# Block-sorted attention with a gated MLP on one core: q and the attention output turned by DMA transposes

## The chip, the core and the metric

The kernel runs on one core of a Trainium2 chip. A core has five engines with an instruction queue each: PE (TensorE, matrix products, with its weight loads listed apart as PEld), DVE (VectorE), ACT (ScalarE), POOL (GpSimd) and SP (SyncE, here for starting DMAs only). Sixteen DMA engines move data between the device's memory (HBM) and the core's SBUF. PE writes its results to PSUM, 8 banks of 2 KB on each of 128 partitions, and DVE or ACT copy them out to SBUF. The metric is the device time of one execution in microseconds (us), less is better.

An engine works through its queue in order. An instruction that waits for a semaphore holds up all that stands behind it on the same engine, a DMA start on SP or POOL included.

## The reference

Four batches, eight heads, 768 positions, 64 numbers a head. A small matrix per head and batch, made doubly stochastic by five rounds, mixes the eight blocks of 96 positions of k and v; each block then attends within itself. The heads together are the input x of a gated MLP (gMLP).

```
def _attn_ref(q, k, v, sort_net) -> np.ndarray:
    ...
    P = sort_net
    for _ in range(5):
        P = P - np.max(P, axis=-1, keepdims=True)
        P = np.exp(P)
        P = P / (np.sum(P, axis=-1, keepdims=True) + 1e-09)
        P = P / (np.sum(P, axis=-2, keepdims=True) + 1e-09)
    ...
    k_sorted = np.einsum('bhij,bhjcd->bhicd', P, k_b).reshape(B, H, S, D)
    v_sorted = np.einsum('bhij,bhjcd->bhicd', P, v_b).reshape(B, H, S, D)
    ...
    scores = scale * np.matmul(q_b, k_sb.transpose(0, 1, 2, 4, 3))
    ...
    return np.matmul(attn, v_sb).reshape(B, H, S, D).astype(np.float32)

def _moe_ref(x, w_in, w_spatial, b_spatial, w_out) -> np.ndarray:
    h = np.maximum(x @ w_in, 0.0)
    u, v = (h[..., :d_ff // 2].copy(), h[..., d_ff // 2:].copy())
    ...
    v_n = (v - mu) / np.sqrt(var + 1e-06)
    v_s = np.einsum('ts,bsd->btd', w_spatial, v_n) + b_spatial[None, :, None]
    gated = u * v_s
    return (gated @ w_out).astype(np.float32)
```

Here B = 4, H = 8, S = 768, D = 64, d_model = 512 and d_ff = 1024. Inputs and output are float32; the kernel works in bf16 with float32 sums.

## The kernel before

The work is cut into units, one function `u_XX` each, and a long string ORDER lists their calls. That list alone sets the order of the instructions on every engine: the scheduler is told to keep it. The arguments of a unit follow after colons: usually the PSUM tile, the engine that copies the result out (A for ACT, D for DVE), the batch, the pair of heads, and the half of the blocks. hp is a pair of heads (four in all), ih a half of the eight blocks (384 positions).

The units, in the order of the data:

- L loads: q, k or v of a batch by one DMA on POOL's queue, cast to bf16 on the way, as 128 x 8 pieces of 384 numbers (a partition holds six neighbouring positions of each head); also the weights wv and wu (the two halves of w_in), ws (w_spatial) and wo (w_out). IN loads the sorting matrix by SP, and the first 64 partitions of batch 0's q in float32 (q_raw), which CQ casts on ACT and POOL.
- SK is one of the five normalizing rounds (ACT and DVE in turn), PR, P0, PC and PD spread the result into the mixing matrices pd of each batch, on PE, DVE, ACT and POOL.
- QT turns q of two heads on PE with the identity matrix, 12 products for a batch (ih = 2) or a half of the partitions (ih = 0 or 1), and a copy PSUM to SBUF into qT. KT does the same with pd in the identity's place, which gives the sorted K. VT and VX do batch 0's sorted V; for the others VM forms it, and VC moves it to blocks of 96 rows by eight DMAs on SP (vb from vm).
- SC computes scores of a pair of heads and a half (8 products) and their exponentials on ACT; AT the product with V (8 products) and, on DVE, the division by the row sum, into x_sb, 96 positions to a partition row.
- XT turns two chunks of x_sb by 8 transposes on PE, with a copy by DVE or ACT into xT. A batch needs four XT (two halves, two chunk pairs).
- WS turns w_spatial. VP and UP are the two halves of x @ w_in, LN and LA the normalization, SP the product with w_spatial and the gate (z and gt), OP the last product, with a copy to o_sb and a DMA on SP to the output. BB loads the bias b_bc.
- DM are products of zeros (of the tile warm) on PE early on.

x_sb is a ring of two tiles, qT one of five, the q loads one of two. PSUM is four tiles of two banks; `ps_tile` hands one out:

```
    def ps_tile(n, dt=FP32):
        return psum.tile([128, 2, 512 if dt == FP32 else 1024], dt, name=f"ps{n}", tag=f"ps{n}")
```

A unit that takes tile n waits until the last unit on it has been copied out.

Of the kernel before, what the change touches and what calls it, by code (L numbers as in the profile page):

```python
# [8 lines left out]
FP32 = mybir.dt.float32  # L9
BF16 = mybir.dt.bfloat16  # L10
# [11 lines left out]
QT:3:D:0:2:1 QT:1:A:0:1:1 QT:0:D:0:3:1 VT:2:A:3:1 SC:3:0:1:0 VX:1:D:2:0 AT:0:0:0:0 PD:1:0:4
VT:2:A:3:0 QT:1:A:0:0:1 VT:3:D:0:1 L:q:1:0:128 SC:2:0:1:1 VX:0:D:3:0 L:wo AT:1:0:2:0 VX:3:A:0:1
VX:0:A:3:1 AT:2:0:3:0 VT:3:A:1:1 VT:1:A:2:1 L:v:2:0:128 AT:0:0:1:0 SC:3:0:2:1 XT:2:D:0:0:1 SC:1:0:3:1
XT:0:D:0:0:0 L:k:2:0:128 VX:3:A:1:1 PD:1:4:8 WS:2:D:1 SC:1:0:0:1 WS:0:D:3 VX:3:A:2:1 L:q:2:0:128
WS:2:D:0 AT:1:0:1:1 WS:0:A:5 AT:3:0:0:1 VP:2:D:0:0:1 VM:1:A:1:2 VM:0:A:1:1 UP:3:A:0:0:0 VM:2:D:1:0
VM:1:A:1:3 VP:0:A:0:2 KT:3:A:1:2:2 KT:1:A:1:0:2 AT:2:0:3:1 UP:0:A:0:1:0 AT:3:0:2:1 KT:1:A:1:3:2
# [18 lines left out]
SP:1:D:2:2 AT:2:3:3:0 UP:3:A:3:1:1 UP:0:A:3:0:1 AT:1:3:1:0 SP:3:D:2:0 XT:2:A:3:0:0 XT:0:A:3:0:1
VP:1:A:3:4:5 VP:3:A:3:0:1 VP:2:A:3:2:3 LN:3:4:6 UP:0:A:3:0:0 LA:3:5 UP:1:A:3:1:0 LA:3:4 LN:3:0:4
LA:3:1 OP:3:A:2:1 OP:2:A:2:0 LA:3:2 OP:0:A:2:2 LA:3:3 LA:3:0 SP:1:D:3:2 SP:3:P:3:3 SP:2:D:3:1
SP:0:D:3:0 OP:1:A:3:1 OP:3:D:3:0 OP:2:A:3:2
# [12 lines left out]
def kernel(  # L62
# [12 lines left out]
    nc = tc.nc  # L75
# [3 lines left out]
    BLK = S // NB  # L79
# [44 lines left out]
    q_raw = const.tile([64, H, G * D], FP32, name="q_raw")  # L124
# [33 lines left out]

    def u_L(what, *a):
# [36 lines left out]

    def u_CQ(eng, hp):
        hp = int(hp)
        if ("q", 0) not in st:
            alloc(0, "q")  # L200
        o, i = st["q", 0][0:64, 2 * hp:2 * hp + 2], q_raw[:, 2 * hp:2 * hp + 2]
        if eng == "A":
            nc.scalar.copy(out=o, in_=i)  # L203
        else:
            nc.gpsimd.tensor_copy(out=o, in_=i)  # L205
# [356 lines left out]
```

## Time and profile before

| | us |
|---|---|
| three runs: median (lowest to highest) | 176.13 (174.57 to 176.19) |
| the profiled execution | 175.73 |
| its span, from the first to the last instruction | 173.7 |
| mean granted clock of PE in it | 0.953 of full |

All rows of the profile come from that one execution. Times in rows are microseconds from the start of the span, or mean nanoseconds where a row says so. The page cuts the span into 40 slices and gives the busy share of each engine in tenths, the clock that PE was granted (PEclk) and the DMA engines' share. A row of a group of instructions reads: line, engine, operation, output tile, input tiles and shape, count, then busy time and mean ns of one, then the idle time of the engine just ahead of them and what ended it. The chain of waits follows the work that ended last back through whatever released it; in order of time it lists start, duration and what ran. Matmuls are pipelined, so PE's cost of a unit is read from the chain, which counts from one start to the next, and not from the mean of one.

Sizes of DMAs are given as written to SBUF; a load with a cast reads twice that from HBM. In the row of a DMA issue, the last number is the time from the issue to the landing of the last byte.

### The profile page before, as it was taken

The numbers are of one execution on the slowest core, as the hardware profiler recorded it, in microseconds if no ns is written. First come the engines' busy times: TensorE is split into PE (matmuls) and PEld (weight loads), VectorE is DVE, ScalarE is ACT, GpSimd is POOL, SyncE is SP. The second block draws the span as 40 slices with busy tenths as digits, with TensorE's granted clock in tenths as the row PEclk, the third lists the DMA queues.
The fourth block names the chain that finished last, engine by engine and source line by source line (L and its number), as shares of the span: only waits on it lengthen the run. The fifth ranks groups of instructions, "written<-read, shape, count | busy, mean of one in ns | idle before, by whom it ended". The sixth has DMA issues, their size and how long they took to land.

```text
span 173.7 us, 4271 instructions
## 1 busy us (share of the span) xinstructions
PE 151.8 (87%) x1827; PEld 97.8 (56%) x1838; DVE 120.1 (69%) x252; ACT 93.5 (54%) x140; POOL 34.1 (20%) x42
## 2 busy tenths in 40 slices
PE   0096697999989999999999999999999999999570
PEld 0054586885865785656457556754566655455220
DVE  5277765568778888878876759888767759537420
ACT  4144574557896898043777660738644357620030
POOL 8285940911010000350000017200000000003000
PEclk9999975569999999999999999999999999999996
DMA  3999999999999990189253018100440000170044
GB/s 78 200 204 204 207 213 203 204 204 205 204 250 262 204 180 4 27 137 171 40 207 142 17 16 154 23 0 4 179 183 4 0 0 4 54 283 25 0 184 178
DMA packets 21025, 21.97 MB, mean 126 GB/s; under 512 B 912, under 2 KB 17808, under 8 KB 21008
## 3 DMA queue, kind: packets, MB, share of 16 engines
q0 software_dynamic: 14336, 11.80, 43.3%
q1 hardware_dynamic: 6672, 9.91, 19.9%
q8 instruction: 14, 0.23, 0.5%
q14 instruction: 3, 0.02, 0.0%
HBM read 24.78 MB, written 6.29 MB: 179 GB/s over the span
## 4 chain that ended last, share of the span: by engine, by line
PE 74%; DMA 9%; DVE 9%; issue 3%; ACT 2%; SPq 1%; ACTq 0%; DVEq 0%
PE ps L493 17%; PE ps L440 11%; PE ps L481 11%; PE ps L514 10%; PE ps L399 5%; PE ps L376 5%; DMA q_raw<-in_q_dram 4%; PE ps L303 3%; PE ps L421 3%; DMA vb<-vm 3%; PE ps L288 2%; PE ps L336 2%; PE ps L267 2%; DMA out_dram<-o_sb 2%; PE ps L348 1%
## 5 line engine op out<-in xcount | busy, mean ns | idle before, releaser
L384 ACT ACTIVATE ex<-ps 96x768 bf16<-96x768 f32 x32 | 24.7, 803 | 17.9 <-PE ps L376 17.5
L493 PE MATMUL ps<-wspT,v_sb 128*128 128x384 bf16 x192 | 33.2, 326 | 0.0
L505 POOL TENSOR_TENSOR gt<-z,u_sb 128x768 bf16<-128x768 f32 x6 | 9.8, 1638 | 100.4 <-DVE z L499 76.6
L493 PEld LDWEIGHTS <-v_sb 128*128 128x128 bf16 x192 | 18.1, 98 | 11.5
L514 PE MATMUL ps<-w_out_sb,gt 128*128 128x512 bf16 x92 | 21.7, 379 | 2.3 <-DVE gt L505 2.1
L481 PE MATMUL ps<-xT,w_in_sb 128*128 128x384 bf16 x128 | 23.1, 326 | 0.0
L499 DVE TENSOR_TENSOR z<-ps,b_bc 128x768 f32<-128x768 f32 x16 | 15.3, 955 | 11.3 <-PE ps L493 11.3
L407 DVE TENSOR_TENSOR x_sb<-ps,rec 96x512 bf16<-96x512 f32 x32 | 22.0, 687 | 1.1
L440 PE MATMUL ps<-w_in_sb,xT 128*128 128x512 bf16 x89 | 22.2, 379 | 0.4
L454 DVE BATCH_NORM_STATS2 stats<-v_sb 128x6 f32<-128x512 bf16 x24 | 16.3, 679 | 5.8 <-ACT v_sb L112 5.6
L106 ACT COPY o_sb<-ps 128x1024 f32<-128x1024 f32 x10 | 10.1, 1013 | 18.4 <-PE ps L514 14.3
L112 ACT ACTIVATE u_sb<-ps 128x768 bf16<-128x768 f32 x15 | 12.1, 809 | 7.8 <-PE ps L481 7.4
L514 PEld LDWEIGHTS <-gt 128*128 128x128 bf16 x96 | 9.0, 98 | 12.5 <-DVE gt L505 2.5
L481 PEld LDWEIGHTS <-w_in_sb 128*128 128x128 bf16 x128 | 11.8, 98 | 7.6
L288 PE MATMUL ps<-ident,q_in 128*64 128x128 bf16 (+1 forms) x240 | 8.4, 221 | 8.7 <-POOL q_in L205 8.7
L399 PE MATMUL ps<-vb,ex 96*128 96x65 bf16 x256 | 13.8, 201 | 1.7 <-issue 1.1
L399 PEld LDWEIGHTS <-ex 96*128 96x128 bf16 x256 | 12.1, 103 | 5.0 <-issue 1.9
L440 PEld LDWEIGHTS <-xT 128*128 128x128 bf16 x96 | 8.7, 97 | 9.2
L288 PEld LDWEIGHTS <-q_in 128*64 128x64 bf16 (+1 forms) x240 | 7.0, 120 | 9.6 <-ACT q_in L203 8.7
L376 PEld LDWEIGHTS <-kT 64*96 64x96 bf16 x256 | 8.2, 128 | 4.9 <-issue 3.7
L376 PE MATMUL ps<-qT,kT 64*96 64x96 bf16 x256 | 10.8, 219 | 0.1
L112 ACT ACTIVATE v_sb<-ps 128x1024 bf16<-128x1024 f32 (+1 forms) x9 | 8.4, 928 | 4.6 <-PE ps L440 4.6
(75 smaller groups left out, 200.6 us busy)
## 6 DMA issues: line engine op xcount, KB each, us to landing
out_dram<-o_sb SPq DMA_DIRECT2D x12, 512.0 KB, 2.8
k_in<-in_k_dram POOLq DMA_DIRECT2D x4, 768.0 KB, 17.4
v_in<-in_v_dram POOLq DMA_DIRECT2D x4, 768.0 KB, 14.8
vb<-vm SPq DMA_DIRECT2D x24, 99.0 KB, 2.8
q_in<-in_q_dram POOLq DMA_DIRECT2D x3, 768.0 KB, 18.3
wsp_nat<-in_moe_w_spatial_dram POOLq DMA_DIRECT2D x1, 1152.0 KB, 10.4
w_in_sb<-in_moe_w_in_dram POOLq DMA_DIRECT2D x2, 512.0 KB, 12.6
q_raw<-in_q_dram SPq DMA_DIRECT2D x1, 768.0 KB, 6.6
```

The costliest lines, as they stand in the source:

```text
L112: nc.scalar.activation(out=out, in_=in_, func=AF.Relu)
L288: nc.tensor.matmul(t[hh * 64:hh * 64 + 64, g * n:(g + 1) * n], lhsT=st["q", b][lo:lo + n, 2 * hp + hh, g * D:(g + 1) * D], rhs=ident[lo:lo ...
L376: nc.tensor.matmul(t[0:BLK, hh, ii * BLK:(ii + 1) * BLK], lhsT=kT[rows, i * BLK:(i + 1) * BLK], rhs=qT[rows, i * BLK:(i + 1) * BLK], start ...
L384: nc.scalar.activation(out=e[:, 0:2 * NI * BLK].rearrange("p (h c) -> p h c", h=2), in_=t[0:BLK, :, 0:NI * BLK], func=AF.Exp, scale=scale,)
L399: nc.tensor.matmul(t[:, hh, ii * VW:ii * VW + D + 1], lhsT=e[:, c:c + 128], rhs=vb[b % 2][:, ih * NI + ii, 2 * hp + hh, 0:D + 1], start=Tr ...
L407: nc.vector.tensor_mul(out=x_sb[:, :, hp * 128:hp * 128 + 128].rearrange("p i (h d) -> p h i d", h=2), in0=tv[:, :, :, 0:D], in1=_raw_ap(r ...
L440: nc.tensor.matmul(t[:, x, :], lhsT=st["xT", b][:, kc, n * 128:(n + 1) * 128], rhs=w_in_sb[:, kc, DH:DFF], start=(kc == 0), stop=(kc == KC ...
L454: nc.vector.bn_stats(out=stats, in_=v_sb[:, x, :])
L481: nc.tensor.matmul(t[:, x, 0:HW], lhsT=w_in_sb[:, kc, mc * 128:(mc + 1) * 128], rhs=st["xT", b][:, kc, ih * HW:(ih + 1) * HW], start=(kc = ...
L493: nc.tensor.matmul(t[:, x, 0:HW], lhsT=st["v_sb", b, n][:, mc * 128:(mc + 1) * 128], rhs=wspT[:, n, x * HW:(x + 1) * HW], start=(n == 0), ...
L499: nc.vector.tensor_add(out=z.rearrange("p (x c) -> p x c", x=2), in0=t[:, :, 0:HW], in1=b_bc.rearrange("p (x c) -> p x c", x=2),)
L514: nc.tensor.matmul(t[:, x, :], lhsT=st["gt", b, mc][:, c * 128:(c + 1) * 128], rhs=w_out_sb[:, mc, :], start=(mc == 0), stop=(mc == FC - 1),)
```

## The change

The following is done at once, with a new ORDER for all of it.

- The first half of batch 0's q is loaded by POOL's queue with a cast, as its first DMA (L:q:0:0:64). q_raw and CQ are gone.
- Batch 0's KT takes all 128 partitions in one unit (ih = 2) instead of two halves; PR puts both halves of its product into one bank.
- PSUM is one tile of eight banks, and a unit takes the bank n of its argument and the next. Units that need one bank may take an odd one, and the dependences follow from the banks that are touched.
- For batches 1 to 3, LQ loads q with 64 numbers to a piece, positions on partitions, by eight DMAs on POOL's queue, and QX turns the whole batch by one DMA transpose on SP into qT, which is now one tile for all heads, in a ring of two. The twelve QT of these batches are gone.
- For batches 1 to 3, XX turns a half of x by one DMA transpose on SP into an xT tile for that half (a ring of four). The twelve XT of these batches are gone. Batch 0 keeps XT and QT.
- Copies, gates and loads are spread anew over the engines and the list.

The diff, with a line or two of the list:

```diff
--- before.py
+++ after.py
@@ -14,39 +14,35 @@
 
 
 ORDER = """
-IN ID L:k:0:0:128 MK L:v:0:0:128 SX SK:0 L:wv SK:0 CQ:P:2 CQ:A:3 SK:0 QT:0:A:0:3:0 SK:0 QT:1:A:0:2:0
...
+L:q:0:0:64 ID IN SK:0 L:k:0:0:128 MK SK:0 SX SK:0 QT:0:A:0:1:0 QT:7:A:0:3:0 QT:1:A:0:2:0 SK:0
...
 """
 
 
@@ -98,8 +94,11 @@
     small = ctx.enter_context(tc.tile_pool(name="small", bufs=4))
     psum = ctx.enter_context(tc.tile_pool(name="psum", bufs=1, space=bass.MemoryType.PSUM))
 
+    ps = psum.tile([128, 8, 512], FP32, name="ps")
+    ps_bf = ps.rearrange("p x c -> p (x c)").bitcast(BF16).rearrange("p (x c) -> p x c", x=8)
+
     def ps_tile(n, dt=FP32):
-        return psum.tile([128, 2, 512 if dt == FP32 else 1024], dt, name=f"ps{n}", tag=f"ps{n}")
+        return (ps if dt == FP32 else ps_bf)[:, int(n):min(int(n) + 2, 8)]
 
     def copy(eng, out, in_):
         if eng == "A":
@@ -121,7 +120,6 @@
     p_t = const.tile([BH, 2, BH], BF16, name="p_t")
     sel = const.tile([BH, NI, 128], BF16, name="sel")
     m32 = const.tile([128, TB], FP32, name="m32")
-    q_raw = const.tile([64, H, G * D], FP32, name="q_raw")
     rowsum = const.tile([BH, NB], FP32, name="rowsum")
     colsum = const.tile([BH, NB], FP32, name="colsum")
     b_bc = const.tile([128, S], FP32, name="b_bc")
@@ -156,6 +154,35 @@
             in_=_raw_ap(src, b * H * S * D + lo * G * D, [[G * D, hi - lo], [S * D, H], [1, G * D]]),
         )
 
+    def u_LQ(b):
+        b = int(b)
+        st["q", b] = ld.tile([128, HP, G, 2, D], BF16, name="q_tok", tag="q")
+        for h in range(H):
+            nc.gpsimd.dma_start(
+                out=st["q", b][:, h // 2, :, h % 2],
+                in_=_raw_ap(q, (b * H + h) * S * D, [[D, 128], [128 * D, G], [1, D]]),
+            )
+
+    def u_QX(b):
+        b = int(b)
+        q_tile(b, 0)
+        nc.sync.dma_start_transpose(
+            out=st["qT", b].rearrange("p h (c x) -> p (h c) x", x=128),
+            in_=st["q", b].rearrange("p a c h d -> p (a c h d)"),
+        )
+
+    def u_XX(b, ih):
+        b, ih = int(b), int(ih)
+        nc.sync.dma_start_transpose(
+            out=x_tile(b, ih).rearrange("p k (i c) -> p (k i) c", c=BLK),
+            in_=st["x", b, ih].rearrange("p k i c -> p (k i c)"),
+        )
+
+    def x_tile(b, ih):
+        if ("xT", b, ih) not in st:
+            st["xT", b, ih] = att.tile([128, KC, HW], BF16, name="xT", tag="xT", bufs=4)
+        return st["xT", b, ih]
+
     def u_L(what, *a):
         if what in ("q", "k", "v"):
             load(what, *(int(x) for x in a))
@@ -172,7 +199,6 @@
 
     def u_IN():
         nc.sync.dma_start(out=p_all, in_=sort_net.rearrange("b h i j -> (b h) i j"))
-        nc.sync.dma_start(out=q_raw, in_=_raw_ap(q, 0, [[G * D, 64], [S * D, H], [1, G * D]]))
         nc.vector.memset(warm, 0.0)
         nc.vector.memset(eps_tile, 1e-6)
 
@@ -193,16 +219,6 @@
         nc.vector.tensor_copy(out=mask16, in_=m32)
         for n in range(NE):
             nc.vector.memset(ex[n][:, 2 * NI * BLK:], 0.0)
-
-    def u_CQ(eng, hp):
-        hp = int(hp)
-        if ("q", 0) not in st:
-            alloc(0, "q")
-        o, i = st["q", 0][0:64, 2 * hp:2 * hp + 2], q_raw[:, 2 * hp:2 * hp + 2]
-        if eng == "A":
-            nc.scalar.copy(out=o, in_=i)
-        else:
-            nc.gpsimd.tensor_copy(out=o, in_=i)
 
     def u_IV(n):
         n = int(n)
@@ -226,7 +242,7 @@
                 out=p_t.rearrange("p x y -> p (x y)"), in_=p_bf.rearrange("p i j -> p (i j)"))
 
     def u_PR(ps):
-        st["pr"] = ps_tile(ps)[:, :, 0:NI * BH].rearrange("p x (i y) -> p x i y", i=NI)
+        st["pr"] = ps_tile(ps)[:, 0, 0:NB * BH].rearrange("p (x i y) -> p x i y", x=2, i=NI)
         for ih in range(2):
             for ii in range(NI):
                 nc.tensor.matmul(
@@ -270,9 +286,9 @@
 
 
     def q_tile(b, hp):
-        if ("qT", b, hp) not in st:
-            st["qT", b, hp] = att.tile([128, S], BF16, name="qT", tag="qT", bufs=5)
-        return st["qT", b, hp]
+        if ("qT", b) not in st:
+            st["qT", b] = att.tile([128, HP, S], BF16, name="qT", tag="qT", bufs=2)
+        return st["qT", b][:, hp]
 
     def k_tile(b, hp):
         if ("kT", b, hp) not in st:
@@ -390,7 +406,7 @@
     def u_AT(ps, b, hp, ih):
         b, hp, ih = int(b), int(hp), int(ih)
         if ("x", b, ih) not in st:
-            st["x", b, ih] = att.tile([BLK, NI, DM], BF16, name="x_sb", tag="x", bufs=2)
+            st["x", b, ih] = att.tile([BLK, KC, NI, 128], BF16, name="x_sb", tag="x", bufs=2)
         e, x_sb = st["e", b, hp, ih], st["x", b, ih]
         t = ps_tile(ps)
         for hh in range(2):
@@ -405,27 +421,25 @@
         rec = small.tile([BLK, 2, NI], FP32, name="rec", tag="rec")
         nc.vector.reciprocal(out=rec, in_=tv[:, :, :, D])
         nc.vector.tensor_mul(
-            out=x_sb[:, :, hp * 128:hp * 128 + 128].rearrange("p i (h d) -> p h i d", h=2),
+            out=x_sb[:, hp].rearrange("p i (h d) -> p h i d", h=2),
             in0=tv[:, :, :, 0:D],
             in1=_raw_ap(rec, 0, [rec.ap[0], [NI, 2], [1, NI], [0, D]]),
         )
 
     def u_XT(ps, eng, b, ih, kp):
         b, ih, kp = int(b), int(ih), int(kp)
-        if ("xT", b) not in st:
-            st["xT", b] = att.tile([128, KC, S], BF16, name="xT", tag="xT", bufs=2)
         t = ps_tile(ps, BF16)
         for x in range(2):
             kc = 2 * kp + x
             for ii in range(NI):
                 nc.tensor.transpose(
                     t[:, 0, x * HW + ii * BLK:x * HW + (ii + 1) * BLK],
-                    st["x", b, ih][:, ii, kc * 128:(kc + 1) * 128],
+                    st["x", b, ih][:, kc, ii, :],
                     ident[0:BLK, 0:BLK],
                 )
         copy(
             eng,
-            st["xT", b][:, 2 * kp:2 * kp + 2, ih * HW:(ih + 1) * HW],
+            x_tile(b, ih)[:, 2 * kp:2 * kp + 2],
             t[:, 0, 0:S].rearrange("p (x c) -> p x c", x=2),
         )
 
@@ -439,7 +453,7 @@
             for kc in range(KC):
                 nc.tensor.matmul(
                     t[:, x, :],
-                    lhsT=st["xT", b][:, kc, n * 128:(n + 1) * 128],
+                    lhsT=x_tile(b, n // 3)[:, kc, n % 3 * 128:(n % 3 + 1) * 128],
                     rhs=w_in_sb[:, kc, DH:DFF],
                     start=(kc == 0), stop=(kc == KC - 1),
                 )
@@ -480,7 +494,7 @@
             for kc in range(KC):
                 nc.tensor.matmul(
                     t[:, x, 0:HW], lhsT=w_in_sb[:, kc, mc * 128:(mc + 1) * 128],
-                    rhs=st["xT", b][:, kc, ih * HW:(ih + 1) * HW],
+                    rhs=x_tile(b, ih)[:, kc],
                     start=(kc == 0), stop=(kc == KC - 1),
                 )
         relu(eng, st["u", b, m][:, :, ih * HW:(ih + 1) * HW], t[:, :, 0:HW])
```

On SP's queue, from the first copies of v to the first outputs, stood this before (vb is the sorted v of a batch in blocks, vm the same before the move):

```order
L363 DMA vb1_99<-vm1_97 96x1x528 x8
L180 DMA b_bc_82<-in_moe_b_spatial_dram 128x768
L363 DMA vb0_98<-vm0_96 96x1x528 x8
L522 DMA out_0_dram<-o_sb_1741 128x2x512
L522 DMA out_0_dram<-o_sb_1753 128x2x512
L522 DMA out_0_dram<-o_sb_1810 128x2x512
```

and this stands there now (q_tok is a batch's q as LQ loads it, x_sb a half of the attention output):

```order
L169 DMA_TRANSPOSE qT_889<-q_tok_814 128x24x128
L379 DMA vb1_99<-vm1_97 96x1x528 x8
L206 DMA b_bc_82<-in_moe_b_spatial_dram 128x768
L169 DMA_TRANSPOSE qT_1043<-q_tok_947 128x24x128
L379 DMA vb0_98<-vm0_96 96x1x528 x4
L176 DMA_TRANSPOSE xT_1202<-x_sb_998 128x16x96
L379 DMA vb0_98<-vm0_96 96x1x528 x4
L176 DMA_TRANSPOSE xT_1355<-x_sb_1107 128x16x96
L536 DMA out_0_dram<-o_sb_1473 128x2x512
L169 DMA_TRANSPOSE qT_1490<-q_tok_1278 128x24x128
L536 DMA out_0_dram<-o_sb_1502 128x2x512
```

The transposes of q stand ahead of the copies of v for the same batch, and the transpose of batch 2's q (the fourth row) stands ahead of those of batch 1's x.

On POOL's queue, from batch 1's q to batch 2's, stood this before:

```order
L154 DMA q_in_601<-in_q_dram 128x8x384
L171 DMA w_out_sb_90<-in_moe_w_out_dram 128x4x512
L154 DMA v_in_686<-in_v_dram 128x8x384
L154 DMA k_in_741<-in_k_dram 128x8x384
L251 TENSOR_TENSOR pd1_93<-mask16_84,prep_sb_91 128x512
L154 DMA q_in_782<-in_q_dram 128x8x384
```

and this stands there now:

```order
L161 DMA q_tok_814<-in_q_dram 128x6x64 x8
L198 DMA w_out_sb_90<-in_moe_w_out_dram 128x4x512
L152 DMA v_in_829<-in_v_dram 128x8x384
L152 DMA k_in_831<-in_k_dram 128x8x384
L267 TENSOR_TENSOR pd2_94<-mask16_84,prep_sb_91 128x512
L161 DMA q_tok_947<-in_q_dram 128x6x64 x8
```

A load of q that was one DMA of 1024 pieces is now eight of 768 each, at the same place in the sequence.

More of the change, by code (lines that the diff above doesn't have):

```diff
@@ L22 @@
[L22 to L27, printed above, removed]
@@ L46 @@
[L46 to L49, printed above, removed]
+L:q:0:0:64 ID IN SK:0 L:k:0:0:128 MK SK:0 SX SK:0 QT:0:A:0:1:0 QT:7:A:0:3:0 QT:1:A:0:2:0 SK:0
+QT:0:A:0:0:0 DM:7:6:384 SK:1 DM:0:6:384 DM:7:2:384 PR:0 P0:0:4:8 L:v:0:0:128 P0:1:4:8 P0:0:0:4
```

49 lines of the change are left out of this document (27 added, 22 removed).

## The prediction

> **What bounds the kernel now.** I read the page's slices first, then the chain in order of time, the instructions in order of time around two places, and the DMA views.
>
> ```profile
> span 173.7 us, 4271 instructions
> PE 151.8 (87%) x1827; PEld 97.8 (56%) x1838; DVE 120.1 (69%) x252; ACT 93.5 (54%) x140; POOL 34.1 (20%) x42
> ...
> PE   0096697999989999999999999999999999999570
> ...
> PEclk9999975569999999999999999999999999999996
> DMA  3999999999999990189253018100440000170044
> GB/s 78 200 204 204 207 213 203 204 204 205 204 250 262 204 180 4 27 137 171 40 207 142 17 16 154 23 0 4 179 183 4 0 0 4 54 283 25 0 184 178
> ...
> PE 74%; DMA 9%; DVE 9%; issue 3%; ACT 2%; SPq 1%; ACTq 0%; DVEq 0%
> ```
>
> A slice is 4.34 us. Two resources are full, one after the other: the DMA engines from about 4 to 63 us (9 in every slice, some 204 GB/s as written), and PE from there to about 153 us. PE's clock was granted at about half between 23 and 37 us. So work taken off PE counts in full only behind the loads; ahead of that a late tensor decides. The profiled execution took 175.73 us, 2.03 more than its span; the median of the three runs is 176.13, 0.4 above it, and my sum is made against the 175.73.
>
> **PE's unit costs**, from the chain in order of time (start, duration, what). L421 turns x, L288 q, L303 forms sorted K, L376 scores, L399 attention, L348 sorted v, L481 UP, L440 VP, L493 SP, L514 OP.
>
> ```profile
> 53.13 1.73 PE ps L440 x8
> ...
> 69.14 1.95 PE ps L493 x12
> ...
> 88.47 1.30 PE ps L481 x8
> 89.77 0.49 PE ps L376 x16
> ...
> 93.99 0.68 PE ps L421 x16
> 94.67 1.13 PE ps L303 x36
> 95.79 0.34 PE ps L288 x12
> ...
> 97.53 0.24 PE ps L399 x8
> 97.78 0.33 PE ps L348 x2
> ...
> 121.56 1.73 PE ps L514 x8
> ```
>
> One QT or XT unit is 0.34 us of PE (12 or 8 instructions). Removed are 12 of each for batches 1 to 3: 24 x 0.34 = 8.2 us. Eight half K units of batch 0 become four whole ones, worth about 1 us; nineteen warm-up matmuls stand where ten stood, in PE's idle start.
>
> With them go PSUM copies:
>
> ```profile
> L106 ACT CAST qT<-ps 128x768 bf16<-128x768 f32 (+1 forms) x12 | 7.7, 660 | 0.8 <-PE ps L288 0.7
> L108 DVE CAST qT<-ps 128x768 bf16<-128x768 f32 (+1 forms) x8 | 6.2, 796 | 2.3 <-PE ps L288 2.3
> L108 DVE COPY xT<-ps 128x768 bf16<-128x768 bf16 x11 | 5.9, 554 | 1.5 <-PE ps L421 1.3
> L106 ACT COPY xT<-ps 128x768 bf16<-128x768 bf16 x5 | 3.8, 801 | 3.8 <-PE ps L421 3.8
> ```
>
> 24 copies of 0.55 to 0.8 us leave DVE and ACT. Neither is full (69% and 54%), so this and the eight PSUM banks, which let one-bank units run ahead, I cost at nothing; PE's matmuls cover it.
>
> **The start.** q's first half moves from SP's queue, with a cast behind it, to POOL's queue, ahead of k. From the chain, then POOL's instructions in order of time, then the view of the tile k_in:
>
> ```profile
> 1.19 6.63 DMA q_raw<-in_q_dram
> 7.84 0.83 ACT q_in L203
> ```
> ```profile
> 1.43 1.06 POOL L154 DMA_DIRECT2D k_in<-in_k_dram  x1
> ```
> ```profile
> DMA to landing us min/median/max: 9.7/17.4/21.0
> ```
>
> The first k, issued at 1.43 us on an idle queue, lands 9.7 us later; its own 1024 pieces take 3.9 us of that (below). A half q of 512 pieces issued at 0.7 us then lands 9.7 - 1.9 us later, at 8.5, against 7.84 + 0.83 = 8.67 for landing and cast now. Sinkhorn starts its fourth round where it started its third, so it ends perhaps half a microsecond earlier. I count zero, since loads decide further on; but the 1.9 us are added to POOL's queue, while SP's idle one no longer carries them.
>
> **The loads.** Batches 1 to 3 of q now come as 8 DMAs each, 128 x 6 pieces of 64 elements: 6144 pieces of 128 B as written, against 1024 of 768 B. No row shows such pieces, so I bound them by two sizes that do run. First two stretches of the span, then POOL's issues in order of time, the view of the tile q_in, and the page's DMA issues (the last number is us to landing):
>
> ```profile
> core 0: us, PE busy (x) PEld busy (x) DVE busy (x) ACT busy (x) POOL busy (x), PEclk, DMA share, GB/s
> 23.00:27.00 4.00, 3.64 (x79) 3.15 (x74) 2.66 (x6) 3.05 (x6) 0.53 (x1) 0.65 1.16 211
> 30.00:36.00 6.00, 6.00 (x77) 5.24 (x74) 3.37 (x7) 3.84 (x7) 4.85 (x5) 0.50 1.32 204
> ```
> ```profile
> 18.15 0.89 POOL L169 DMA_DIRECT2D wsp_nat<-in_moe_w_spatial_dram  x1
> ...
> 33.26 0.94 POOL L154 DMA_DIRECT2D q_in<-in_q_dram  x1
> ```
> ```profile
> DMA to landing us min/median/max: 9.3/14.0/24.9
> ```
> ```profile
> wsp_nat<-in_moe_w_spatial_dram POOLq DMA_DIRECT2D x1, 1152.0 KB, 10.4
> ...
> out_dram<-o_sb SPq DMA_DIRECT2D x12, 512.0 KB, 2.8
> vb<-vm SPq DMA_DIRECT2D x24, 99.0 KB, 2.8
> ...
> b_bc<-in_moe_b_spatial_dram SPq DMA_DIRECT2D x1, 384.0 KB, 8.0
> ```
>
> w_spatial, 768 pieces of 1536 B, lands at 28.5 us and moves alone in the first window: 16 x 1536 B / 211 GB/s = 116.5 ns a piece on an engine. k, v and q fill the second: 16 x 768 / 204 = 60.2 ns. The line through both gives 3.9 ns plus 56.3 ns for 768 B, so 13.3 ns for 128 B, and 6144 x 13.3 / 16 = 5.1 us a batch where the old form took 1024 x 60.2 / 16 = 3.85. Ends: bytes alone, 3.85 us; each small piece at the price of a 768 B one, 23 us. POOL's issue is another floor: a 768-piece DMA took 0.89 us (w_spatial's), so 8 cost 7.1, though they are issued ahead of the data. The 24 issues are 21 us of POOL, which is 80% idle; behind the last eight stand only two gt of batches 1 and 2. I take 5.1, since both measured sizes lie on a line that bytes explain almost wholly: 1.25 us more a batch.
>
> Batch 2's q, issued at 33.26 us, is the 24.9 us case and lands at 58.2 now. Afterwards: 58.2 + 1.9 (half q in this queue) - 0.7 (queue begins earlier) + 2 x 1.25 = 61.9 us.
>
> The Trainium skill ("DMA: Bandwidth & Descriptors", Specifications) asks for 512 B or more per transfer for line rate. It speaks against this change; it gives no factor, and no row here has such a load, so it only raises the chance of the second rival.
>
> **The transposes.** QX turns 768 KB, XX 384 KB, on SP's queue, each at once. No row has one. Lower end: a plain 512 KB store lands in 2.8 us, so by bytes 4.2 for QX and 2.1 for XX. Upper end: b_bc's 384 KB took 8.0 us beside the loads, so 8.0 for XX and 16 for QX. QX:2 runs beside the loads of v3 and k3; at half of 204 GB/s its 768 KB need 7.7 us. I take 6.5 for QX and 4.0 for an XX, nearer to the lower end, because the loads leave the engines free soon after.
>
> The order on SP puts xT of batch 1 behind the q of batch 2, which waits for a load. UP:0:A:1:0:0 needs that xT and has only two score units (0.5 us) between itself and QX:2's landing. With the engines shared, XX:1:0 lands 3.4 us after QX:2: a new wait of 2.9 us. The other XX have PE work between the attention that ends their input and their first reader: about 4.6 us for XX:2:1 (one OP, four AT, one SP), 6.1 for XX:3:1, 6.9 for XX:3:0 and 8.3 for XX:2:0, each less 1.2 for x's own scaling. XX:1:1 comes 4.0 us behind XX:1:0 on the same queue, and 4.5 us of UP, K, v and AT units stand between their readers. At 4.0 us only XX:2:1 is late, by 0.6. Also queued behind QX:1 and QX:2 are the vb copies of batches 1 and 2; their readers, AT, follow scores that wait for the same transpose.
>
> **The sum.** Let S be the start of batch 2's first scores. From PE's instructions in order of time:
>
> ```profile
> 75.73 0.56 PE L376 MATMUL ps<-qT,kT 64*96 64x96 bf16 x16
> ```
> ```profile
> 162.77 5.35 PE L514 MATMUL ps<-w_out_sb,gt 128*128 128x512 bf16 x23 [2.11 <-DVE gt L505]
> ```
>
> Now S is 75.7 and PE ends at 168.1, 92.4 us later. Counting units from there in the old list gives 88.7 us of work (13 SP 25.4, 12 OP 20.8, 11 UP 14.3, 16 VP tiles 13.9, 16 SC and 16 AT 7.7, 9 XT, 4 QT, 4 KT, 3 VM 6.8), so 3.7 us are waits, 2.1 of them the gt before the last OP. In the new list: 12 SP 23.4, 12 OP 20.8, 12 UP 15.6, 18 VP tiles 15.6, SC and AT 7.7, 6 KT 2.0, 4 VM 1.3: 86.4 us. The same 3.7 of waits stand, since the list still ends on four SP and three OP.
>
> S = 61.9 + 0.1 + 6.5 = 68.5 us. Ahead of S the new list has 42.2 us of units; from 8.5 us, with 3.1 of warm-up and some 7 for a half-granted clock, PE is through by 61, so the load does set S. Total: 68.5 + 86.4 + 3.7 + 2.9 + 0.6 + 7.6 (PE's end to the end of the execution, 175.73 - 168.1) = 169.7, so **170 us**, 6 below now. Ends of this case: bytes alone and QX 4.2, XX 2.1 give S 63.7 and 163; POOL's 7.1 us a batch, QX 8 and 1 us more of XX waits give S 73.9 and 176.
>
> **Rivals.**
> First, slower: the transposes become the bound, at UP and VP behind each XX and at the scores behind each QX. With b_bc's price (QX 16, XX 8): S = 78.0, the wait on XX:1:0 7.5, the others 4.6 + 0.9 + 3.1 + 2.3 = 10.9: 78.0 + 86.4 + 3.7 + 7.5 + 10.9 + 7.6 = 194. Halfway (QX 10, XX 6) about 179; it decides from XX near 5.5 us on. For it: six XX lie on the way of single readers. Against: 384 KB is little beside 204 GB/s.
>
> The Trainium skill disagrees with itself here. "VectorE: DVE Perf Modes" (The three transpose paths) lists 390 ns for a 128 x 128 transpose on TensorE and 1309 ns by DMA: one after another, 24 make a 31 us QX and 16 a 21 us XX, an estimate of some 270 us. But 16 turns took 0.68 us in the chain above, 43 ns each, so its times are not rates. "Advanced Engine Details and Errata" (X-Bar Transpose) says as fast as regular DMAs: that is the lower end, about 165.
>
> Second, slower: small pieces cost more than bytes. At 24 ns a piece a batch takes 9.2 us, 5.4 more than now; q of batch 2 lands at 70.2, S is 76.7 and the time 178. At 60 ns it is 206. For it: nothing here runs so small from HBM. Against: the line's 3.9 ns.
>
> Third, no change: waits at S eat what PE saves. With S = 74.5, halfway to the second rival, 175.7.
>
> **Chances.** Forecast 0.56 (163 to 174.4), no change 0.12, slow transposes 0.20, small pieces 0.12. A measurement of this kernel tells about 1% from no change, 174.4 to 177.9 us. So faster 0.56, same 0.12, slower 0.32. The range, 163 to 186 us, leaves out the upper half of the first rival, the far end of the second and a little below; the forecast's own is 163 to 176.
>
> **What would show it.** S in the new trace (first scores of batch 2) near 68.5, with PE waiting on a DMA there and again before the first UP of batch 1; q's third load landing near 62; QX at 6 to 7 us from issue and XX near 4; PE with 12 instructions of 96-row turns and no q turns behind the loads. Repeated PE waits on xT would mean the first rival, a load phase to 80 us the second.

## The result, and the profile after

| | before | after |
|---|---|---|
| median of 4 runs each | 176.16 us | 191.44 us |
| lowest to highest | 174.57 to 177.25 | 190.35 to 193.03 |
| ratio, 95% interval | | 1.0907 [1.0788, 1.1027] |
| profiled execution, span | 175.73, 173.7 | 190.35, 188.5 |

The change costs 15 us where 6 were to be gained, and the range reached only to 186. (Medians here and below are of all runs of a kernel, ratios leave out executions that were slowed together with a lower granted clock of TensorE; of both_on_pe a single run of four is left, and its time is given.)

First the page of the changed kernel: span, busy times, the slices of 4.71 us, the chain's shares.

```profile
span 188.5 us, 3792 instructions
PE 145.0 (77%) x1547; PEld 87.5 (46%) x1559; DVE 118.5 (63%) x245; ACT 80.1 (42%) x120; POOL 46.4 (25%) x59
...
PE   0696979997003899802999995999999999999580
...
PEclk9999999999855589965799997999999999999998
DMA  4999999999999999999900599381025540233035
...
PE 52%; DMA 26%; SPq 7%; DVE 6%; POOL 3%; issue 2%; ACT 1%; ACTq 0%; DVEq 0%; POOLq 0%
```

PE is busy 6.8 us less (145.0 for 151.8), not far from the 9 forecast (8.2 of turns and about 1 of K units), yet the span is 14.8 us longer. Two holes are new in PE's row, near 47 to 60 and 80 to 88 us, and the granted clock falls in and behind them. The DMA engines stay full to about 94 us (20 slices) instead of 65 (15 slices of 4.34 us), and DMA holds 26% of the chain instead of 9%. What PE waited for, in all, times, longest:

```profile
PE ps L392 <- DMA qT<-q_tok: 14.7, 2, 13.9
PE ps L495 <- DMA xT<-x_sb: 8.1, 1, 8.1
...
PE ps L528 <- DVE gt L519: 2.3, 1, 2.3
PE ps L454 <- DMA xT<-x_sb: 2.1, 1, 2.1
```

L392 forms scores, L495 is UP, L454 VP. SyncE's queue in order of time shows the transposes (L169 is QX, L176 XX); the tile views of qT and of xT follow, each with its times from issue to landing.

```profile
41.61 11.82 SPq L169 DMA_TRANSPOSE qT<-q_tok  x1
...
66.57 10.77 SPq L169 DMA_TRANSPOSE qT<-q_tok  x1
77.46 2.51 SPq L379 DMA_DIRECT2D vb<-vm  x4
80.07 2.12 SPq L176 DMA_TRANSPOSE xT<-x_sb  x1
...
105.82 4.22 SPq L169 DMA_TRANSPOSE qT<-q_tok  x1
```
```profile
DMA to landing us min/median/max: 6.1/12.9/18.1
```
```profile
DMA to landing us min/median/max: 3.8/4.7/8.0
```

The same 768 KB lands after 18.1 us in batch 1, 12.9 in batch 2 and 6.1 in batch 3. Only the last runs with no load beside it. SyncE itself is held 10.8 to 11.8 us by a QX beside loads, and 4.2 by the free one; the vb copies and XX:1:0 stand behind. PE's instructions at the three waits:

```profile
59.79 0.87 PE L392 MATMUL ps<-qT,kT 64*96 64x96 bf16 x16 [13.95 <-DMA qT<-q_tok]
...
79.48 0.56 PE L392 MATMUL ps<-qT,kT 64*96 64x96 bf16 x16 [0.76 <-DMA qT<-q_tok]
88.15 2.74 PE L495 MATMUL ps<-xT,w_in_sb 128*128 128x384 bf16 x8 [8.11 <-DMA xT<-x_sb]
```

S, the first scores of batch 2, is 79.5 where 68.5 was forecast. PE came to it only 0.76 us before q did: the 14 us lost on batch 1's q had already made PE late. So QX:1 and QX:2 bind here almost together.

### The profile page after: what moved, and what is told of

Same layout as the page of the kernel before. It is cut to its first block, busy times and chain, and to the rows that moved or that the text cites. A ratio compares the mean times of both kernels' runs of the same rounds, so it can differ in the third digit from the quotient of the medians.

```text
span 188.5 us, 3792 instructions
## 1 busy us (share of the span) xinstructions
PE 145.0 (77%) x1547; PEld 87.5 (46%) x1559; DVE 118.5 (63%) x245; ACT 80.1 (42%) x120; POOL 46.4 (25%) x59
## 4 chain that ended last, share of the span: by engine, by line
PE 52%; DMA 26%; SPq 7%; DVE 6%; POOL 3%; issue 2%; ACT 1%; ACTq 0%; DVEq 0%; POOLq 0%
PE ps L507 13%; PE ps L495 9%; PE ps L528 9%; PE ps L454 9%; DMA k_in<-in_k_dram 9%; DMA xT<-x_sb 7%; SPq L169 6%; DMA vb<-vm 4%; PE ps L392 3%; PE ps L415 3%; DMA q_in<-in_q_dram 3%; DMA q_tok<-in_q_dram 3%; DVE z L513 3%; PE ps L276 2%; POOL pd L267 2%; DVE gt L519 2%
## 5 line engine op out<-in xcount | busy, mean ns | idle before, releaser
L495 PE MATMUL ps<-xT,w_in_sb 128*128 128x384 bf16 x128 | 24.4, 338 | 8.1 <-DMA xT<-x_sb 8.1
L454 PE MATMUL ps<-w_in_sb,xT 128*128 128x512 bf16 x88 | 23.1, 396 | 2.7 <-DMA xT<-x_sb 2.1
L519 POOL TENSOR_TENSOR gt<-z,u_sb 128x768 bf16<-128x768 f32 x4 | 6.5, 1635 | 74.8 <-DVE rec L422 74.8
L161 POOL DMA_DIRECT2D q_tok<-in_q_dram x24 | 20.0, 855 | 16.6 <-DMA k_in<-in_k_dram 7.5
L392 PE MATMUL ps<-qT,kT 64*96 64x96 bf16 x256 | 11.1, 224 | 15.1 <-DMA qT<-q_tok 14.7
L111 ACT ACTIVATE u_sb<-ps 128x768 bf16<-128x768 f32 x14 | 11.4, 811 | 21.6 <-PE ps L495 20.6
L495 PEld LDWEIGHTS <-w_in_sb 128*128 128x128 bf16 x128 | 12.3, 100 | 17.0 <-DMA xT<-x_sb 8.2
L107 DVE CAST vm<-ps 128x768 bf16<-128x768 f32 x4 | 3.8, 958 | 26.0 <-PE ps L364 15.2
L105 ACT COPY o_sb<-ps 128x1024 f32<-128x1024 f32 x11 | 11.1, 1012 | 18.2 <-PE ps L528 15.0
L392 PEld LDWEIGHTS <-kT 64*96 64x96 bf16 x256 | 8.5, 132 | 20.3 <-issue 18.4
L454 PEld LDWEIGHTS <-xT 128*128 128x128 bf16 x96 | 9.2, 101 | 12.5 <-DMA xT<-x_sb 2.2
L528 PEld LDWEIGHTS <-gt 128*128 128x128 bf16 x96 | 8.8, 98 | 12.2 <-DVE gt L519 2.4
L415 PE MATMUL ps<-vb,ex 96*128 96x65 bf16 x256 | 12.5, 196 | 1.0 <-DMA vb<-vm 0.7
L415 PEld LDWEIGHTS <-ex 96*128 96x128 bf16 x256 | 10.9, 99 | 4.1 <-issue 1.5
L111 ACT ACTIVATE v_sb<-ps 128x1024 bf16<-128x1024 f32 (+1 forms) x6 | 5.7, 953 | 16.3 <-PE ps L454 16.2
## 6 DMA issues: line engine op xcount, KB each, us to landing
v_in<-in_v_dram POOLq DMA_DIRECT2D x4, 768.0 KB, 12.4
```

Of the source, the lines that this page charges most:

```text
L111: nc.scalar.activation(out=out, in_=in_, func=AF.Relu)
L161: nc.gpsimd.dma_start(out=st["q", b][:, h // 2, :, h % 2], in_=_raw_ap(q, (b * H + h) * S * D, [[D, 128], [128 * D, G], [1, D]]),)
L392: nc.tensor.matmul(t[0:BLK, hh, ii * BLK:(ii + 1) * BLK], lhsT=kT[rows, i * BLK:(i + 1) * BLK], rhs=qT[rows, i * BLK:(i + 1) * BLK], start ...
L415: nc.tensor.matmul(t[:, hh, ii * VW:ii * VW + D + 1], lhsT=e[:, c:c + 128], rhs=vb[b % 2][:, ih * NI + ii, 2 * hp + hh, 0:D + 1], start=Tr ...
L454: nc.tensor.matmul(t[:, x, :], lhsT=x_tile(b, n // 3)[:, kc, n % 3 * 128:(n % 3 + 1) * 128], rhs=w_in_sb[:, kc, DH:DFF], start=(kc == 0), ...
L495: nc.tensor.matmul(t[:, x, 0:HW], lhsT=w_in_sb[:, kc, mc * 128:(mc + 1) * 128], rhs=x_tile(b, ih)[:, kc], start=(kc == 0), stop=(kc == KC ...
```

## Experiments

Twelve kernels. Each table or line gives the median and the ratio to the kernel before, measured in the same rounds, with its interval; two were run once only.

### Which half of the change costs the time

**both_on_pe** takes every DMA transpose of q and x out, **q_big_on_pe** those of q alone, **x_on_pe** those of x alone. Units that return stand ahead of their readers, in places that I chose, and one or two of their neighbours take another PSUM bank.

```diff
 # q_big_on_pe (both_on_pe alike), for batches 1 to 3
-LQ:1 ... QX:1
+L:q:1:0:128 ... QT:4:A:1:3:2 QT:0:D:1:1:2 ... QT:4:D:1:2:2 QT:6:A:1:0:2
 # both_on_pe and x_on_pe, for both halves of batches 1 to 3
-XX:1:0
+XT:1:A:1:0:0 ... XT:2:A:1:0:1
```

**q_small_on_pe** keeps q's small pieces and turns them on TensorE.

```diff
-QX:1
+QZ:4:A:1:3 QZ:0:D:1:1 ... QZ:4:D:1:2 QZ:6:A:1:0
...
+    def u_QZ(ps, eng, b, hp):
+        b, hp = int(b), int(hp)
+        t = ps_tile(ps, BF16)
+        for g in range(G):
+            nc.tensor.transpose(t[:, 0, g * 128:(g + 1) * 128], st["q", b][:, hp, g].rearrange("p h d -> p (h d)"), ident)
+        copy(eng, q_tile(b, hp), t[:, 0, 0:S])
```

> All 12 q turns and 12 x turns of batches 1 to 3 are back on TensorE, and q is loaded in large pieces; the start, the whole K products and the eight banks stay as changed. Theory one (the transposes on SyncE lost the time, above all those of q beside the loads): about the time before, 176 us, 172 to 180. Theory two (the new start, the order of the list or the banks lost it): 184 us or more, little below the changed kernel's 191.

> Only q goes back: large pieces and turns on TensorE; the six DMA transposes of x stay. Theory one (the q transposes beside the loads are the loss): no waits on qT, XX near 4 us each with nothing of 12 us ahead of it on SyncE, so most of the 15 us come back: 172 to 178 us. Theory three (the transposes of x with their single readers are the loss): 183 us or more, with PE waiting on xT again and again.

> As the run with q back on TensorE, but q still comes in 128-byte pieces, 8 DMAs a batch, and TensorE turns it with 6 instructions of 128 columns a unit. Theory one: the pieces cost 13.6 ns each by the trace, some 1.2 us a batch, so at most 4 us above the run with large pieces, and still below 180 us. Theory four (the small pieces and POOL's eight issues are the loss): 8 us or more above it, 184 us or more.

> Only x goes back to TensorE; q's small pieces and the three transposes of q stay on SyncE. Theory one: the idle 14 us before batch 1's scores and the late first scores of batch 2 stay, the 8.1 us wait on XX:1:0 goes, 12 turns of 0.34 us come back: 183 to 189 us. Theory three (the transposes of x): 178 us or less.

| kernel | q turned by | x turned by | us | ratio |
|---|---|---|---|---|
| changed | SyncE | SyncE | 191.44 | 1.0907 [1.0788, 1.1027] |
| x_on_pe | SyncE | TensorE | 188.52 | 1.0769 [1.0588, 1.0949] |
| q_big_on_pe | TensorE | SyncE | 174.86 | 0.9955 [0.9891, 1.0018] |
| q_small_on_pe | TensorE, small pieces | SyncE | 175.15 | 1.0005 [0.9944, 1.0066] |
| both_on_pe | TensorE | TensorE | 179.65 (one run) | |

All four came out where theory one had put them, both_on_pe by its one run. Taking the q transposes out brings 16 to 17 us back; taking those of x out brings 3. So the q transposes are the loss. The small pieces are not: 175.15 and 174.86 are apart by less than the intervals allow. Why both_on_pe stands above the kernel before is taken up under the list below.

### SyncE's order, or the loads beside

**xx_first** changes only SyncE's order; **held** keeps loads away from QX:1 and QX:2 by a small copy on POOL that reads the turned q, with QX:1 moved up to stand right behind LQ:1.

```diff
 # xx_first
-QX:2 SC:2:1:1:0 ... XX:1:0
+SC:2:1:1:0 ... XX:1:0 QX:2
 # held
-LQ:1 ... L:wo L:v:2:0:128 L:k:2:0:128 ... QX:1 ... L:v:3:0:128
+LQ:1 QX:1 ... HO:1 L:wo L:v:2:0:128 L:k:2:0:128 ... HO:2 L:v:3:0:128
...
+    def u_HO(b):
+        nc.gpsimd.tensor_copy(out=hold[:, int(b):int(b) + 1], in_=st["qT", int(b)][:, 0, 0:1])
```

> Only the order on SyncE's queue: QX:2 is issued behind XX:1:0, where it stood three steps ahead of it. Theory one (loads and transposes share the DMA engines): XX:1:0 goes out near 71 us, as soon as x is there, and its 8.1 us wait on PE goes; QX:2 then goes out near 73 us, behind the last loads of k and v, and lands 6 to 8 us after its issue, so batch 2's first scores stay near 80 us; in all 181 to 186 us. Theory five (SyncE's order is the whole loss): 178 us or less. Theory six (a q transpose takes 12 us or more wherever it stands): first scores of batch 2 at 85 us or later, 187 us or more.

> A one-element copy on POOL that reads the turned q stands ahead of the loads that were issued beside QX:1 (w_out, v2, k2, q2) and one ahead of those beside QX:2 (v3, k3), so that both transposes run with no load beside them. Theory one: QX:1 and QX:2 land 5.5 to 8 us after their issue, as QX:3 did with 6.1, against 18.1 and 12.9; the first scores of batch 1 start near 49 us, not 60. The loads come later by what they were held, so the time gains little: 180 to 190 us. Theory six (the size, or the first transposes of a program, make it slow): 11 us or more for both.

xx_first: 192.19 us, 1.0958 [1.0875, 1.1041]. held: 194.29 us, 1.1034 [1.0935, 1.1134]. Both missed the forecast of their time, upwards. The landings, from the tile views, did what theory one said: in xx_first (qT, then xT), then in held (qT):

```profile
DMA to landing us min/median/max: 5.5/6.1/19.0
```
```profile
DMA to landing us min/median/max: 3.8/5.1/11.2
```
```profile
DMA to landing us min/median/max: 5.5/6.1/7.3
```

With the loads held, all three q transposes land in 5.5 to 7.3 us, the first of the program among them. Neither size nor coldness makes them slow; the loads do. The time does not follow, because somebody still runs beside the loads. PE's waits in order of time, first xx_first, then held:

```profile
81.34 0.56 PE L393 MATMUL ps<-qT,kT 64*96 64x96 bf16 x16 [1.96 <-DMA qT<-q_tok]
94.32 1.06 PE L455 MATMUL ps<-w_in_sb,xT 128*128 128x512 bf16 x2 [6.07 <-DMA xT<-x_sb]
```
```profile
62.69 0.80 PE L369 MATMUL ps<-v_in,pd 128*128 128x384 bf16 x2 [13.03 <-DMA v_in<-in_v_dram]
91.95 2.74 PE L500 MATMUL ps<-xT,w_in_sb 128*128 128x384 bf16 x8 [11.18 <-DMA xT<-x_sb]
```

In xx_first QX:2 goes out free and the 8.1 us wait on XX:1:0 is gone, but S stays late, at 81.3, and now XX:1:1, issued at 82.7 beside q's last load, makes PE wait 6.1 us. In held PE waits 13.0 us for v2, and XX of batch 1 runs beside the late v3 and k3 and costs 11.2. Batch 1's first scores did start near 49 us (48.96), as forecast. SyncE's order is not the loss: with it changed the time stays.

### How the DMA engines are shared

The DMA view of short windows counts packets by queue: q0 carries the loads, q1 SyncE's transfers. The first window, held from 44 to 46 us, has a QX alone. The second, the changed kernel from 50 to 52, has QX:1 beside loads of 768-byte pieces; the third, from 56 to 58, QX:1 beside q's 128-byte pieces.

```profile
DMA packets 1693, 0.43 MB, mean 217 GB/s; under 512 B 1693, under 2 KB 1693, under 8 KB 1693
...
q1 hardware_dynamic: 1693, 0.43, 117.0%
```
```profile
q0 software_dynamic: 375, 0.29, 91.4%
q1 hardware_dynamic: 371, 0.09, 35.9%
```
```profile
q1 hardware_dynamic: 832, 0.21, 81.0%
q0 software_dynamic: 830, 0.10, 79.3%
```

A transpose moves in packets of 0.43 MB / 1693, some 256 bytes. Alone it passes 1693 in 2 us. Beside a load both queues move the same number of packets, whatever their size: 375 to 371, 830 to 832. That they take turns one by one, the rule from here on, can be seen where little moves. From 49.4 to 49.8 us the changed kernel has four packets of each queue, and the view's row in slices of 10 ns gives each by itself, 77 GB/s for 768 bytes and 26 for 256:

```profile
GB/s 77 0 0 0 0 0 26 0 0 0 0 0 77 0 0 0 0 0 26 0 0 0 77 0 0 0 0 26 0 0 0 0 0 77 0 0 0 0 0 26
```

A 256-byte packet that waits for one of 768 bytes gets a quarter of the bytes. One QX is 768 KB / 256 B = 3072 packets; at 371 in 2 us they need 16.6 us, at 1693 only 3.6.

The pace is not all. The changed kernel from 41.61 us, where QX:1 is issued, to 45.6:

```profile
q0 software_dynamic: 909, 0.77, 124.9%
q1 hardware_dynamic: 1, 0.00, 0.0%
```

Beside loads a QX moves its first packet only 4.0 us after its issue (QX:1 and QX:2 alike), alone after 1.2 to 1.8 (held's QX:1 and QX:2, the changed kernel's QX:3). What fills the 4.0 us no run shows. So the 18.1 us of QX:1 are 4.0 of start, 8.4 at the slow pace (1338 packets), 4.8 at the pace beside q's small pieces (the other 1734) and 1.0 to the landing. The 12.9 of QX:2 are 4.0, then 6.6 beside the load of k3 (1264 packets), 1.8 alone (the other 1808) and 0.5 to the landing. In both there is a good half microsecond, around 49.5 and 75.1 us, in which the engines together move next to nothing; its cause is open too.

The rule is shown for transposes beside loads. Where SyncE's queue carries the vb copies, in packets of 1056 bytes, the counts differ: xx_first from 84 to 86 us has 1098 packets of q's load to 207 of SyncE's. SyncE starts these copies one at a time, 96 packets each, and whether its queue had packets ready all the time isn't known.

The Trainium skill ("DMA: Bandwidth & Descriptors", Queues, rings and completion order) says that an engine goes round its queues packet by packet, and that a packet typically holds 9 to 17 descriptors. The trace agrees with the turns, but in the row above they change after every single packet that the profile records, and no run here shows longer ones.

**two_queues** and **ws_again** were to test that rule.

```diff
 # two_queues, in u_QX
-        nc.sync.dma_start_transpose(
+        for eng, lo in ((nc.sync, 0), (nc.scalar, HP // 2)):
+            eng.dma_start_transpose(
 # ws_again
-L:v:3:0:128
+L:ws L:ws L:v:3:0:128
```

> Each QX in two halves of 384 KB, one issued by SyncE, one by ScalarE, all else as changed. Theory one in its sharper form (beside loads each queue gets one packet in turn, so a 256-byte transpose packet waits for a load packet of 768 bytes): two queues of transposes get two packets of three; QX:1 lands 10 to 14 us after issue instead of 18.1. Theory seven (the transposing itself, or the bytes, set the pace): 17 us or more, as with one queue. ScalarE waits for q ahead of its other work, so the time of the kernel says little: 185 to 207 us.

> As the changed kernel, with w_spatial loaded twice more into the same place, unchanged data, on POOL's queue ahead of v3: 1536 packets of 1536 bytes beside QX:2. If each queue gets one packet in turn: where both run, 16 x 2000 / (116.5 + 25.1) = 226 packets of each queue in 2 us, where 768-byte loads left the transposes 371, and QX:2 lands 17 us or more after its issue. If the engines are shared by bytes or by time: 371 packets in 2 us or more, and QX:2 lands in 13 us or less. The time of the kernel is some 10 us above the changed kernel's, since v3 and k3 come later.

two_queues (one run, 196.82 us, inside its forecast) tells nothing of the rule. ScalarE's queue in order of time:

```profile
56.10 1.49 ACTq L171 DMA_TRANSPOSE qT<-q_tok  x1
```

SyncE's half was issued at 39.7 us, ScalarE's only at 56.1: in the built program it waits for the semaphore of SyncE's half, so the two never ran together. The halves of QX:1 landed 15.6 and 10.6 us after their own issues.

ws_again (one run, 197.51 us), from 71.8 to 73.2 us, with QX:2 beside w_spatial's 1536-byte pieces:

```profile
q0 software_dynamic: 158, 0.24, 94.5%
q1 hardware_dynamic: 155, 0.04, 21.5%
```

155 in 1.4 us are 221 in 2 us, where 226 were forecast from the rule and 371 or more from a share of bytes or time. The forecast of the landing (17 us or more) failed: 13.4 us, because the second copy of w_spatial waited for the first to land, and QX:2 ran alone for a while. Its time, forecast some 10 us above the changed kernel's 191, came out 6 above. The rule rests on the counts.

### The list, the start, and a faster kernel

**old_list** is the list of before on the changed code, with q's first half on POOL's queue; **old_list_xx** puts six XX into it, each behind the last attention of its half.

```diff
 # old_list, against the kernel before
-IN ID L:k:0:0:128 ... CQ:P:2 CQ:A:3 ... CQ:P:1 CQ:P:0
+L:q:0:0:64 ID IN L:k:0:0:128
 # old_list_xx, against old_list
-XT:4:D:1:1:1 XT:4:D:1:0:1 XT:2:D:1:0:0 ... XT:0:A:1:1:0
+XX:1:0 ... XX:1:1
```

> The order of the kernel before with all its turns on TensorE and q in large pieces, but with q's first half on POOL's queue ahead of k, one PSUM tile and the new layouts of x and qT: the new start alone, with the old list. If the start costs nothing, as the prediction had it: 174 to 178 us. If it is what made the run with both turns back slow (183.4): 181 us or more.

> As old_list, with the 12 x turns of batches 1 to 3 replaced by six DMA transposes, each directly behind the last attention that fills its input; nothing else in the list is moved to give them time. If the transposes of x gain by themselves: 4 us below old_list or more. If what counts is the place of their readers: UP and VP follow at once in the old list, PE waits on xT two or more times, and the time is within 3 us of old_list.

old_list: 173.63 us, 0.9875 [0.9810, 0.9940]. old_list_xx: 184.03 us, 1.0475 [1.0405, 1.0546]; both forecasts missed, the loss is larger than either had it. PE waits on xT:

```profile
PE ps L457 <- DMA xT<-x_sb: 11.1, 3, 7.0
```

The new start costs nothing, rather gains a little. Six transposes of x in a list without room for them cost 10 us. The waits for them make 11.1, and the longest, 7.0, is for one that goes out at 59.2 us beside the loads of v3 and k3 and takes 10.4; so this is in part the same effect as with q. In the changed list, which leaves room, they cost nothing that shows (q_big_on_pe, 174.86, ratio 0.9955). both_on_pe, with the changed list and no transposes at all, stands 6 us above old_list, by its one run. That would say that the order of the changed list is made for transposes and is worse without them; how much of it is my placing of the returned XT units these runs don't show.

**qx3_only** is q_small_on_pe with batch 3's q back on SyncE, behind the loads; **old_list_qx3** does the same in old_list.

```diff
 # qx3_only, against q_small_on_pe
-XX:1:1 ... QZ:2:A:3:1 ... QZ:4:A:3:3 ... QZ:2:A:3:0 ... QZ:0:A:3:2
+XX:1:1 QX:3
 # old_list_qx3, against old_list
-L:k:3:0:128 ... OP:4:A:0:0 ... L:q:3:0:128 ... QT:6:D:3:0:2 ... QT:2:A:3:3:2 QT:6:A:3:2:2 ... QT:4:D:3:1:2
+L:k:3:0:128 LQ:3 ... OP:4:A:0:0 QX:3
```

> TensorE turns the q of batches 1 and 2 as in the run with small pieces; only batch 3's q is transposed by SyncE, directly behind XX:1:1, when no load runs any more. Theory one: it lands about 6 us after its issue, long before its scores, and 4 turns of about 0.3 us and their copies leave TensorE, so 1 to 3 us below that run: 172 to 175 us, and below the kernel before. Theory six: it lands 12 us or more after its issue and XX:2:1 behind it waits: 176 us or more.

> As old_list, but q of batch 3 comes in small pieces behind k3 and is transposed by SyncE behind batch 1's first outputs, when no load runs; the 4 turns of batch 3 leave TensorE. Theory one: the transpose lands about 6 us after its issue, ahead of its readers, and 4 x 0.34 = 1.4 us go: 172 to 173 us against old_list's 173.6. If what leaves TensorE there is filled by other waits: 173.6 or more. Worse than 176 only if the transpose is late.

qx3_only: 172.34 us, 0.9801 [0.9734, 0.9869]; old_list_qx3: 173.00 us, 0.9863 [0.9790, 0.9937]. In qx3_only the transpose goes out at 85.0 us and lands 5.5 later, and PE no longer waits on qT. It has the lowest median here, some 3 us below q_small_on_pe, at the upper end of what was expected and with intervals that don't touch; that is more than the four turns, 4 x 0.3, and the rest isn't explained. In old_list the same step can't be told from no gain (0.9863 against 0.9875), and the intervals of these two overlap with qx3_only's.

## Why the prediction was wrong, point by point

- **The price of a QX, the step that failed.** The prediction gave it 6.5 us, between 4.2 and 16, by bytes: "at half of 204 GB/s its 768 KB need 7.7 us", and "the loads leave the engines free soon after". Measured are 18.1 and 12.9 beside loads. Two parts of the price failed. It had no term for the 4.0 us to the first packet: 4.0 of start, the 7.7 and 0.5 to the landing would have made 12.2, an estimate near QX:2's 12.9, where 6.5 was taken. And the engines are shared by packets, so a transpose in 256-byte packets gets a quarter beside 768-byte pieces, not half, which is most of what QX:1's 18.1 has above those 12.2. The loads, slowed by it in turn, ran on instead of leaving the engines free. 6.5 is what a QX takes with no load beside it (5.5 to 7.3).
- **QX:1 had no term.** "PE is through by 61, so the load does set S": PE came to S at 79.48 - 0.76 = 78.7, 17.7 late. Of this, 13.95 us are the idle time before batch 1's scores, 0.66 a wait for the vb copies behind QX:1 on SyncE, and about 3.0 the lower clock behind the hole (granted 0.50 while PE was busy for 6.01 us; columns are PE's busy time and instructions, those of PEld, DVE, ACT and POOL, the granted clock, DMA share and GB/s):

```profile
59.80:66.60 6.80, 6.01 (x70) 3.69 (x69) 3.46 (x6) 4.09 (x6) 0.87 (x1) 0.50 1.72 229
```

  So with QX:2 at 6.5 us and QX:1 as it was, S would still have been near 78.7. The prediction priced only the transpose that its sum ran through.
- **S.** Forecast 61.9 + 0.1 + 6.5 = 68.5. Measured 66.6 for QX:2's issue, right behind q's landing at 66.3, and 12.9 for QX:2: 79.5, 11.0 late. Of the 4.7 by which QX:2 went out late, about 4 go with QX:1, which took every second packet ahead of q: in q_small_on_pe, the same loads with no QX, the last of the eight DMAs of batch 2's q goes out at 56.02 us and lands 6.2 later, at 62.2, close to the 61.9 forecast; in the changed kernel it goes out at 55.73 and takes 10.5. First its row and its landing in q_small_on_pe, then its landing in the changed kernel:

```profile
56.02 0.82 POOL L163 DMA_DIRECT2D q_tok<-in_q_dram  x1 [5.96 <-DMA k_in<-in_k_dram]
q_tok<-in_q_dram POOLq DMA_DIRECT2D x1, 96.0 KB, 6.2
```
```profile
q_tok<-in_q_dram POOLq DMA_DIRECT2D x1, 96.0 KB, 10.5
```

- **XX.** 4.0 us each was about right where no load runs (3.8 to 4.9, four of them). XX:1:0 and XX:1:1, beside q's last load, took 8.0 and 7.8; the wait for XX:1:0 was 8.1 instead of 2.9, that for XX:1:1 none. XX:2:1, one of the free ones, took 4.9 and made PE wait 2.1 instead of 0.6.
- **The rest.** From S to the end of the execution the forecast was 86.4 + 3.7 + 2.9 + 0.6 + 7.6 = 101.2; it was 190.35 - 79.48 = 110.9. Of the 9.7, 5.2 and 1.5 are these waits. The remaining 3 are put down to a lower clock, of which 1.7 can be read off: 3.85 us right behind the second hole ran at 0.57. In the hole and behind it (columns as above):

```profile
80.00:88.15 8.15, 0.04 (x3) 0.01 (x1) 0.78 (x1) 1.45 (x2) 5.96 (x8) 0.57 2.08 150
88.15:92.00 3.85, 3.85 (x30) 1.88 (x32) 0.38 (x1) 0.81 (x1) 0.00 (x0) 0.57 1.95 195
```

11.0 + 9.7 make the 20.7 us between 169.7 and the profiled 190.4.

- **The small pieces were right.** 13.3 ns a piece was forecast. The changed kernel from 36 to 38 us, with q's load alone, moves 2397 in 2 us, 16 x 2000 / 2397 = 13.35 ns:

```profile
q0 software_dynamic: 2397, 0.30, 239.5%
```

- **The start** was costed at zero; old_list puts it, with the layouts and the PSUM tile, at 1.2% to the good. The first turn began at 6.50 us, not 8.5, as PE's row shows:

```profile
6.50 1.63 PE L304 MATMUL ps<-ident,q_in 64*64 64x64 bf16 x48 [6.50 <-DMA q_in<-in_q_dram]
```

- **Two readings.** The load phase before ends near 65 us (15 full slices; the last of these loads, k of batch 3, landed at 47.58 + 18.37 = 65.95), not 63; S and the sum do not hang on it. For the third rival S = 74.5 is called halfway to the second rival's 76.7; halfway from 68.5 is 72.6, and 74.5 is what 175.7 needs.
- **The rivals.** The first rival came out nearest (S 78.0, time 194), at a chance of 0.20. Its place was right only in part: it let all six XX be slow, and just those beside loads were. "384 KB is little beside 204 GB/s" was the argument against it, and it was an argument by bytes again. The rule of the Trainium skill that a transpose is as fast as other DMAs ("Advanced Engine Details and Errata", X-Bar Transpose) fits a QX alone, 217 GB/s in the window above where loads alone move 204 to 211, and not one beside loads.

## What to carry to other kernels

A transfer that starts while another queue is busy is to be priced by packets in turn, with the packet size of each, and with a start of its own, and not by a share of the bytes. Work moved from a compute engine to DMA paid here only once the loads were over: for batch 3's q in the changed list (172.34 against 175.15), while for x the runs speak both ways (3 us lost in the changed kernel, some 5 gained in q_big_on_pe if both_on_pe's one run holds). And each copy of a moved step needs its own price, also those that the sum does not run through, since the first of them can make everything behind it late.

## What the runs showed of the hardware

- Two DMA queues, loads and transposes, moved equal numbers of packets: 375 and 371, 830 and 832, 158 and 155, at 768, 128 and 1536 bytes against 256; in a row of 10 ns slices they alternate one for one.
- A DMA transpose of 768 KB landed in 5.5 to 7.3 us alone and in 12.9 to 19.9 beside loads (the longest in ws_again). Its first packet moved 1.2 to 1.8 us after the issue alone, and 3.9 to 4.1 beside loads. It held SyncE's queue for 3.5 to 4.3 us alone, and for 9.0 to 12.4 beside loads.
- 128-byte pieces cost 13.35 ns each on an engine, where a twelfth of a 1536-byte piece is 116.5 / 12 = 9.7.
- TensorE's granted clock was 0.57 in the 8 us in which PE idled for XX:1:0 and in the 3.9 us of work right behind, and 0.50 in the 6.8 us of work behind the first hole.
